# First sequence of a spectral-filter and SwiGLU kernel: filter units moved ahead, last units cut in halves

## The chip, the cores and the metric

The kernel runs on one core of a Trainium2 chip. The metric is the device time of one execution in microseconds; lower is better. Two figures are used side by side: the median of the timed runs, and the time of the one execution that was profiled, whose trace is read here. Times inside the trace count from the start of the profiled span.

Five engines work in parallel, each through its own instructions in order: PE (TensorE, matmuls and transposes by matmul), DVE (VectorE), ACT (ScalarE), POOL (GpSimd) and SP (SyncE). POOL and SP also issue the DMAs of this kernel. PE results land in PSUM banks, which DVE or ACT copy out.

## The reference

For each of 8 sequences of 3008 rows and 256 channels: a real FFT along the sequence, a product with a complex filter, the inverse FFT; then, row by row, an RMS norm and a SwiGLU feed-forward layer with 1536 hidden channels.

```python
X = np.fft.rfft(x, axis=1)
F = (filt_r + 1j * filt_i)[None, :, :]
y = np.fft.irfft(X * F, n=x.shape[1], axis=1)       # 8 x 3008 x 256
x = y.reshape(24064, 256)
rms = np.sqrt(np.mean(x * x, axis=-1, keepdims=True) + 1e-06)
xn = x / rms * rms_g
g = xn @ w_gate                                     # 256 -> 1536
out = (g * (1.0 / (1.0 + np.exp(-g))) * (xn @ w_val)) @ w_out
```

## The kernel before, in words

**The transform.** 3008 is 47 times 64, so the FFT is done in two steps with small tables: step A over 64 points (table `wa`), step B over 47 points with one table for each of 32 residues (`wb`), the filter product, and the same two steps back (`wi`, then `wai`). All are matmuls. Two channel halves of 128 are called `dh`; a "unit" of step B is four residues of one half, so a sequence has 16 units, i = 2g + dh.

**The eight sequences.** The feed-forward work `gv` and `down` (L548 to L565) is a list of 576 items in order. The transforms of sequence b+1 are put between the items of sequence b by a planner with a load table. Sequence 0 has nothing to hide behind: its transform, the loading of the filter and the loading of the weights are written out by hand, in the order in which each engine gets them, and the first item starts after them. The change lies in this hand-written part alone. The planner's items are the same in both kernels.

**The hand-written part, in its order.**

1. POOL issues the DMAs: four for `x` of sequence 0, six of 512 KB for the filter (`f_load`, tile `fs`; for each of three blocks i the imaginary part f=0, then the real part f=1), then `wb` in one call, `wi`, the weights. From the ninth DMA on, each POOL issue waits for the landing of the DMA eight before it. The weights' staging tiles share four buffers with `fs`.
2. Step A: `a0_unit`, six groups for two halves; ACT copies one half from bank tag "pg", DVE the other from "pv". Between them stand `fill` matmuls, whose result is not used, and a transpose of the norm's gain into `gsb`.
3. `tr0_unit(g)`, g = 0 to 7: eight PE transposes and one DVE copy into `t2`. After each of the first seven, one `f_unit`.
4. `f_unit(i, f, dh)`: four PE transposes of one filter tile into a bank, then four copies (five for the last block, i = 2, with one more transpose for the last filter row, tile `tail`) into the filter table `ff`. Twelve units: units 0 to 6 on ACT inside the loop over g, units 7 to 11 behind it, in turn on DVE and ACT. Their order is i, then f, then dh.
5. `f_neg` on POOL writes the negated imaginary part into `ff`, in three pieces, with weight DMAs between them.
6. The loop over p: `b_unit` (PE, banks "mx" and "mb" in turn) and two products `s_part` on DVE with `ff` (L233, L236); two steps later `yt0_unit` (PE, bank "pg", copied out by ACT); two steps later `bi_unit` (PE, bank "pv", copied into `uu` by ACT). For the last unit, i = 15, both copies are on DVE, each of a whole unit, one after the other.
7. `t4_first` transposes the first four row groups of `uu` (PE, copied by ACT and DVE), SP issues the DMA transposes `t4_load`, and `first_norm` computes the first norm: step A back (`psn`), squares on ACT, column sums on PE (`psq`), square root on ACT (`u`), reciprocal on DVE (`rho`), a broadcast by PE (`psr`) and the product `xn` on DVE, in two halves h. Then ACT loads its table for Silu, and item (0, 0, 0) starts. It is itself in two halves.

The waits are made by a framework that watches tiles. It also keeps two engines from touching one PSUM bank at once: in `first_norm` the DVE copy of `psn` waits for the ACT square of the same bank.

Of the kernel before, what the change touches and what calls it, by code (L numbers as in the profile page):

```python
# [12 lines left out]
AXT = mybir.ActivationFunctionType  # L13
# [7 lines left out]
P = 128  # L21
D = 256
# [3 lines left out]
H = 24  # L26
K2 = 32
SL = 48
KR = 2 * SL
# [71 lines left out]
def kernel(  # L101
# [11 lines left out]
    nc = tc.nc  # L113
# [4 lines left out]
    wb_d = nc.inline_tensor(wb_np, name="wb_t").ap()  # L118
# [29 lines left out]
    idf = glob.tile([P, P], FP32)  # L148
    wb = glob.tile([P, K2, KR], FP16)
# [4 lines left out]
    ff = glob.tile([P, 2, K2, 3 * SL], FP32)  # L154
# [3 lines left out]
    gsb = glob.tile([P, 2], FP32)  # L158
    hhs = [glob.tile([P, 512], FP16, name="hh%d" % i) for i in range(4)]
    ss3 = [glob.tile([P, 4, 2, P], FP16, name="ss%d" % i) for i in range(3)]  # L160
    ones = glob.tile([P, 1], FP16)
    epsb = glob.tile([P, 1], FP32)
# [28 lines left out]
    def bank(i, name):  # L191
        pool, tag = ((psM, "mx"), (psG, "pg"), (psV, "pv"), (psB, "mb"))[i]
        return pool.tile([P, 512], FP32, tag=tag, name=name)

    def copy(eng, out, in_, scale=None):
        if eng == "A":
            nc.scalar.activation(out=out, in_=in_, func=AXT.Copy, **({} if scale is None else {"scale": scale}))  # L197
        elif scale is None:
            nc.vector.tensor_copy(out=out, in_=in_)
        else:  # L200
            nc.vector.tensor_scalar(out=out, in0=in_, scalar1=scale, scalar2=None, op0=ALU.mult)
# [77 lines left out]

    done = [0] * B  # L280

    def bi_unit(b, i, eng="A", bk=0):
        g, dh = divmod(i, 2)
        yt = st[b]["yt"][g]
        ps = bank(bk, "psi")[:, 0:4 * KR].rearrange("p (k j) -> p k j", k=4)
        for k in range(4):
            nc.tensor.matmul(ps[:, k, :], yt[0:KR, k, dh, :], wi[0:KR, 4 * g + k, :], start=True, stop=True)  # L287
        dst = uu[:, :, dh, 16 * g:16 * g + 16].rearrange("p c (k m) -> p c k m", k=4)
        copy(eng, dst, ps.rearrange("p k (c m) -> p c k m", c=H))
        done[b] += 1  # L290
        if done[b] == K2 // 2:
            half = uu[:, H - 1, :, :].rearrange("p e (k m) -> p e k m", k=K2)
            if b % 2:
                nc.gpsimd.tensor_copy(out=half[:, :, :, 2:4], in_=left)
            else:
                nc.gpsimd.tensor_copy(out=left, in_=half[:, :, :, 0:2])
# [89 lines left out]
    def f_unit(i, f, dh, e):  # L386
        t = fst[i]
        ps = bank(1 + "AV".index(e), "psf").rearrange("p (a q) -> p a q", a=FR4)
        for a in range(FR4):
            nc.tensor.transpose(ps[:, a, :], t[:, f, a, ds(dh * P, P)], idf)  # L390
        v = ps.rearrange("p a (q s) -> p s a q", s=16)
        fk = ff[:, dh].rearrange("p (t k) c -> p t k c", k=4)
        lo = SL * (1 + f) + 8 * i
        hi = lo + H
        if i < 2:
            copy(e, fk[:, :, :, lo:lo + 8], v[:, 0:8])
            copy(e, fk[:, ::-1, 1:4, hi:hi + 8][:, :, ::-1, :], v[:, 8:16, 1:4, :])
            copy(e, fk[:, 1:8, 0, hi:hi + 8][:, ::-1, :], v[:, 9:16, 0, :])
            copy(e, ff[:, dh, 0, hi:hi + 8], v[:, 8, 0, :])
        else:  # L400
            nc.tensor.transpose(ps[:, 0, 0:1], tail[0:1, f, ds(dh * P, P)], idf[0:1, 0:1])
            copy(e, fk[:, :, :, lo:lo + 8], v[:, 8:16])
            copy(e, fk[:, ::-1, 1:4, hi:hi + 7][:, :, ::-1, :], v[:, 0:8, 1:4, 1:8])
            copy(e, fk[:, 1:8, 0, hi:hi + 7][:, ::-1, :], v[:, 1:8, 0, 1:8])
            copy(e, ff[:, dh, 0, hi:hi + 7], v[:, 0, 0, 1:8])
            copy(e, ff[:, dh, 0, hi + 7:hi + 8], v[:, 0, 0, 0:1])

    def f_neg(k0, n):
        for dh in range(2):
            nc.gpsimd.tensor_scalar(out=ff[:, dh, k0:k0 + n, 0:SL], in0=ff[:, dh, k0:k0 + n, SL:2 * SL],  # L410
                                    scalar1=-1.0, scalar2=1.0, op0=ALU.mult, op1=ALU.mult)

    def yt0_unit(i, eng, bk):
        g, dh = divmod(i, 2)
        s = st[0]["s"].pop(i)[1]
        ps = bank(bk, "psy")[0:KR].rearrange("p (k t) -> p k t", k=4)
        for k in range(4):
            for e in range(2):
                nc.tensor.matmul(ps[:, k, :], s[e][:, k, :], ident, start=(e == 0), stop=(e == 1))  # L419
        if g not in st[0]["yt"]:  # L420
            yt_tile(0, g)
        copy(eng, st[0]["yt"][g][0:KR, :, dh, :], ps)

    def fill(n):
        ps = bank(0, "pf")
        for _ in range(n):
            nc.tensor.matmul(ps, wa, ss3[0].rearrange("p k e q -> p (k e q)")[:, 0:512], start=True, stop=True)

    def t4_first():
        t = xtp.tile([P, 4, D], FP16, tag="xt", name="t4f")  # L430
        for h in range(2):
            ps = psO.tile([P, 2, 2, P], FP16, tag="po%d" % h, name="pst4")
            for q in range(2):
                for dh in range(2):
                    nc.tensor.transpose(ps[:, q, dh, :], uu[:, 2 * h + q, dh, :], ident)
            copy("AV"[h], t[:, 2 * h:2 * h + 2, :].rearrange("p q (e d) -> p q e d", e=2), ps)
        st[0]["t4f"] = t

    def first_norm():
        xn = xnp.tile([P, 4, 2, P], FP16, tag="xn", name="xn")  # L440
        sq = xtp.tile([P, 4, D], FP16, tag="xt", name="sq").rearrange("p (a e) d -> p a (e d)", a=2)
        y = y_tile()
        psn = [bank(1 + h, "psn") for h in range(2)]
        for h in range(2):
            for q in (2 * h, 2 * h + 1):
                for dh in range(2):
                    nc.tensor.matmul(psn[h][:, ts(2 * (q % 2) + dh, P)], st[0]["t4f"][:, q, ds(dh * P, P)], wai,
                                     start=True, stop=True)
            nc.scalar.activation(out=sq[:, h, :], in_=psn[h], func=AXT.Square)
        copy("V", y[:, 0, :], psn[0])  # L450
        fill(1)
        ps = psB.tile([P, 4], FP32, tag="mb", name="psq")
        for q in range(4):
            for dh in range(2):
                nc.tensor.matmul(ps[:, q:q + 1], sq[:, q // 2, ts(2 * (q % 2) + dh, P)], ones,
                                 start=(dh == 0), stop=(dh == 1))
            if q == 1:
                fill(1)
        u = up.tile([P, 4], FP32, tag="u", name="u")
        rho = up.tile([P, 4], FP32, tag="rho", name="rho")  # L460
        nc.scalar.activation(out=u, in_=ps, func=AXT.Sqrt, scale=1.0 / D, bias=epsb)
        nc.vector.reciprocal(out=rho, in_=u)
        copy("A", y[:, 1, :], psn[1])
        fill(2)
        for h in range(2):
            psr = psO.tile([P, 2, P], FP32, tag="po%d" % h, name="psr")
            for q in range(2):
                nc.tensor.transpose(psr[:, q, :], rho[:, 2 * h + q:2 * h + q + 1].to_broadcast([P, P]), idf)
            nc.vector.tensor_tensor(out=xn[:, 2 * h:2 * h + 2],
                                    in0=psr.unsqueeze(2).to_broadcast([P, 2, 2, P]),  # L470
                                    in1=y[:, h, :].rearrange("p (q e t) -> p q e t", q=2, e=2), op=ALU.mult)
        nc.scalar.activation(out=warm, in_=mhalf, func=AXT.Silu)
        fill(2)
        st[0]["xn"][0] = xn

    def n_first(m):
# [135 lines left out]
    with tc.manual_schedule():  # L612
# [12 lines left out]
        nc.sync.dma_start(tail[0:2, 2, 0:P], moe_rms_g.rearrange("(a p) -> a p", p=P))  # L625
        for i in range(3):
            f_load(i)
        nc.gpsimd.dma_start(wb, wb_d)
        nc.gpsimd.dma_start(wi, wi_d)
        w_load(0)  # L630
        w_load(1)
# [7 lines left out]
        def a0(*gqs):  # L639
            for gq in gqs:  # L640
                for dh in range(2):
                    a0_unit(gq, dh, E[dh], 1 + dh)

        a0(0)
        fill(1)
        psg = bank(3, "psg")
        nc.tensor.transpose(psg[:, 0:2], tail[0:2, 2, 0:P], idf[0:2, 0:2])
        copy("V", gsb, psg[:, 0:2])
        fill(1)
        a0(1, 2)  # L650
        fill(2)
        a0(3)
        fill(1)
        a0(4, 5)
        todo = [(i, f, dh) for i in range(3) for f in range(2) for dh in range(2)]
        for g in range(8):
            tr0_unit(g, "V")
            if g < 7:
                f_unit(*todo[g], "A")
        for n, u in enumerate(todo[7:]):  # L660
            f_unit(*u, "VA"[n % 2])
        f_neg(0, 8)
        w_load(2)
        f_neg(8, 8)
# [6 lines left out]
        for q in range(3):  # L671
            w_gain(q)
        UN = K2 // 2
        for p in range(UN + 4):
            if p < UN:
                b_unit(0, p, (0, 3)[p % 2])
                s_part(0, p, 1)
            if 2 <= p < UN + 2:
                yt0_unit(p - 2, "AV"[p - 2 == UN - 1], 1)
            if p >= 4:  # L680
                bi_unit(0, p - 4, "AV"[p == UN + 3], 2)
            if p >= UN + 1:
                fill(1)
        t4_first()
        fill(2)
        for c in range(NXC):
# [166 lines left out]
```

## Time and profile before

| what | value |
| --- | --- |
| timed runs | 871.36, 873.1, 873.5 us; median 873.1 us |
| profiled execution | 872.03 us, span 870.3 us |
| PE busy | 852.1 us, 98% of the span |
| mean granted PE clock | 0.998 |
| first matmul of the first item (L548) | at 47.77 us |

The profiled execution lies 1.07 us under the median, with 1.7 us of it outside the span. PE is busy through nearly the whole span, but not in its first 48 us, which are 5.5% of it: there each engine is at times the one waited for. Reading therefore goes by stages: first the busy time of each engine in each stage, then the order of time inside the stage, asking what the next instruction waited for.

### The profile page before, as it was taken

To read this page: it belongs to the slowest core of one execution; us is meant where nothing else is said; L and a number is where in the kernel's file an instruction comes from. 1 tells how busy PE (TensorE), PEld (TensorE's weight loads), DVE (VectorE), ACT (ScalarE), POOL (GpSimd) and SP (SyncE) were. 2 spreads that over 40 slices of the span, in tenths; PEclk is the share of its full clock that TensorE was granted. 3 is DMA by queue.
4 is the path that set the end of the run, shared out by engine and by line. 5 is a ranking of instruction groups with operands and counts; after the bars stand their busy time and mean duration, and the time that the engine had idled before them with its cause. 6 is when DMAs were issued, how large, how long until landed. Compare 5 with 4: busy or idle time off the path is not lost.

```text
span 870.3 us, 17008 instructions
## 1 busy us (share of the span) xinstructions
PE 852.1 (98%) x6129; PEld 533.0 (61%) x6129; DVE 559.9 (64%) x936; ACT 612.1 (70%) x1352; POOL 295.5 (34%) x340
## 2 busy tenths in 40 slices
PE   6999999999999999999999999999999999999997
PEld 5755666566665566666566666666666666665664
DVE  5856765776666666666576666667666766555554
ACT  4787777787577766877578765788567865777443
POOL 4813841454143421444034430443214440132000
PEclk9999999999999999999999999999999999999999
DMA  9986678655976666744656666634474331522101
GB/s 283 270 149 156 119 152 191 147 117 139 188 146 124 126 134 131 146 110 101 143 120 136 125 124 136 148 87 92 122 142 92 72 91 43 109 67 49 62 25 49
DMA packets 198605, 107.98 MB, mean 124 GB/s; under 512 B 158966, under 2 KB 182904, under 8 KB 198520
## 3 DMA queue, kind: packets, MB, share of 16 engines
q1 hardware_dynamic: 189896, 85.52, 44.4%
q0 software_dynamic: 8480, 21.24, 12.2%
q8 instruction: 48, 0.79, 0.4%
q14 instruction: 37, 0.30, 0.1%
q10 hardware_dynamic: 144, 0.13, 0.0%
HBM read 45.78 MB, written 35.65 MB: 94 GB/s over the span
## 4 chain that ended last, share of the span: by engine, by line
PE 93%; DVE 2%; DMA 2%; ACT 2%; issue 1%; POOL 0%; POOLq 0%; ACTq 0%
PE po L565 27%; PE pg L548 27%; PE pv L548 26%; PE psb L243 3%; PE psi L287 2%; PE psn L316 2%; PE psa L208 2%; DMA xc<-in_x_dram 1%; PE psy L419 1%; DVE hh L553 1%; DMA yt<-ss 1%; ACT sg L552 1%; PE psf L390 1%; ACT uu L197 0%; PE pst L369 0%
## 5 line engine op out<-in xcount | busy, mean ns | idle before, releaser
L553 DVE TENSOR_TENSOR hh<-pv,sg 128x512 f16<-128x512 f32 (+2 forms) x578 | 391.5, 678 | 289.1 <-ACT sg L552 221.7
L552 ACT ACTIVATE sg<-pg 128x512 f16<-128x512 f32 (+2 forms) x578 | 337.7, 585 | 220.1 <-PE pg L548 215.6
L548 PE MATMUL pg<-xn,wg 128*128 128x512 f16 (+2 forms) x1156 | 337.9, 374 | 0.1
L548 PE MATMUL pv<-xn,wv 128*128 128x512 f16 (+2 forms) x1156 | 337.8, 374 | 0.0
L565 PE MATMUL po<-wo,hh 128*128 128x256 f16 x2256 | 332.5, 272 | 0.0
L565 PEld LDWEIGHTS <-hh 128*128 128x128 f16 x2256 | 213.5, 98 | 108.0 <-issue 4.6
L548 PEld LDWEIGHTS <-wv 128*128 128x128 f16 x1156 | 113.0, 98 | 130.6
L270 POOL TENSOR_TENSOR ss<-s,s 128x384 f16<-128x384 f16 x112 | 101.8, 910 | 247.9 <-DVE s L236 220.7
L548 PEld LDWEIGHTS <-wg 128*128 128x128 f16 x1156 | 111.5, 98 | 17.2 <-issue 0.6
L342 POOL TENSOR_TENSOR xt<-y,rho 128x1024 f16<-128x1024 f32 (+1 forms) x46 | 85.3, 1854 | 2.9
L324 ACT ACTIVATE junk<-y 128x256 f16<-128x256 f32 x180 | 74.3, 413 | 2.8
L233 DVE TENSOR_TENSOR s<-psb,ff 128x384 f16<-128x384 f32 x124 | 67.8, 547 | 1.0 <-PE psb L243 0.9
L236 DVE TENSOR_TENSOR s<-psb,ff 128x384 f16<-128x384 f32 x124 | 67.8, 547 | 0.0
L197 ACT ACTIVATE uu<-psi 128x384 f16<-128x384 f32 x127 | 62.0, 489 | 1.9 <-PE psi L287 1.2
L197 ACT ACTIVATE y<-psn 128x512 f32<-128x512 f32 (+1 forms) x95 | 55.7, 588 | 4.3
L332 POOL TENSOR_SCALAR u<-ss 128x4 f32<-128x4 f32 (+1 forms) x46 | 8.8, 192 | 133.8 <-ACT junk L324 133.5
L287 PEld LDWEIGHTS <-yt 96*128 96x128 f16 x512 | 35.5, 98 | 27.9 <-DMA yt<-ss 1.2
L334 POOL TENSOR_TENSOR rho<-u,mhalf 128x4 f32<-128x4 f32 (+1 forms) x46 | 46.4, 1010 | 3.8
L197 ACT ACTIVATE t<-psa 128x512 f16<-128x512 f32 x71 | 42.1, 596 | 3.3 <-PE psa L208 1.7
L287 PE MATMUL psi<-wi,yt 96*128 96x96 f16 x512 | 43.1, 206 | 0.9 <-DMA yt<-ss 0.8
L243 PE MATMUL psb<-wb,t 96*128 96x96 f16 x480 | 40.5, 208 | 1.9 <-DVE s L236 1.7
L243 PEld LDWEIGHTS <-t 96*128 96x128 f16 x480 | 28.9, 98 | 14.4 <-DVE s L236 5.2
(96 smaller groups left out, 364.5 us busy)
## 6 DMA issues: line engine op xcount, KB each, us to landing
out_dram<-o SPq DMA_DIRECT2D x40, 512.0 KB, 3.5
xc<-in_x_dram POOLq DMA_DIRECT2D x31, 384.0 KB, 5.8
z_tmp<-t SPq DMA_DIRECT2D x28, 384.0 KB, 2.7
t<-z_tmp SPq DMA_DIRECT2D x28, 384.0 KB, 6.1
out_dram<-o SPq DMA_DIRECT2D x7, 384.0 KB, 2.7
fs<-in_filt_i_dram POOLq DMA_DIRECT2D x3, 512.0 KB, 11.4
fs<-in_filt_r_dram POOLq DMA_DIRECT2D x3, 512.0 KB, 11.1
ws<-in_moe_w_gate_dram POOLq DMA_DIRECT2D x3, 512.0 KB, 10.9
```

The costliest lines, as they stand in the source:

```text
L197: nc.scalar.activation(out=out, in_=in_, func=AXT.Copy, **({} if scale is None else {"scale": scale}))
L233: eng.tensor_tensor(out=o, in0=ps, in1=f1, op=ALU.mult)
L236: eng.tensor_tensor(out=o, in0=ps[:, :, ::-1, :], in1=f2, op=ALU.mult)
L243: nc.tensor.matmul(ps[:, ts(k, KR)], st[b]["t2"][kk // KC][:, kk % KC, ds(dh * P, P)], wb[0:KR, kk, :], start=True, stop=True)
L270: nc.gpsimd.tensor_tensor(out=ss3[g % 3][:, :, dh, 0:KR], in0=s[0], in1=s[1], op=ALU.add)
L287: nc.tensor.matmul(ps[:, k, :], yt[0:KR, k, dh, :], wi[0:KR, 4 * g + k, :], start=True, stop=True)
L324: nc.scalar.activation(out=junk, in_=y[:, i, ts(u, D)], func=AXT.Square, accum_out=ss[:, 2 * i + u:2 * i + u + 1])
L342: nc.gpsimd.tensor_tensor(out=xt[:, 0:n, :], in0=y.rearrange("p a (u d) -> p (a u) d", u=2)[:, 0:n, :], in1=rho[:, 0:n].unsqueeze(2).to_br ...
L548: nc.tensor.matmul(ps[:, 0:w], wt[:, dt_, ts(jt, P)], xn[:, q0:q1, dt_, :], start=(dt_ == 0), stop=(dt_ == 1))
L552: nc.scalar.activation(out=sg[:, c], in_=pg[:, 0:w], func=AXT.Silu)
L553: nc.vector.tensor_tensor(out=hh[:, c], in0=pv[:, 0:w], in1=sg[:, c], op=ALU.mult)
L565: nc.tensor.matmul(po[s4 // 2][:, s4 % 2, :], hh[:, ts(s4, P)], wo[:, jt, :], start=(jt == 0 and s4 % 2 == 0), stop=(jt == JT - 1 and (s4 ...
```

## The change

Only the first sequence is touched.

- Two `f_unit`s are issued after step A and ahead of `tr0_unit(0)`; the loop over g then carries units 2 to 8, and units 9, 10, 11 follow it on DVE, ACT, ACT. The last block's order is now dh, then f: both parts of half 0 come before half 1.
- The last filter row is transposed earlier, in step A, into the bank that also takes the gain; one DVE copy puts it into `ff`. `f_unit` loses that transpose and a copy.
- `wb` is loaded by two calls, 16 residues each. One more DMA stands on POOL's queue.
- Unit 15 of `yt0_unit` and of `bi_unit` is cut into two halves of two residues, one copied by DVE and one by ACT. The copy of `bi_unit` 13 moves from ACT to DVE. One `fill` goes, and the two that remain use bank "pg".
- `t4_first` copies its first half on DVE and its second on ACT (before: the other way round).
- `first_norm` takes sums, square root and reciprocal by halves. The fills are placed anew: 2, 1, 1 and 3 of them from `t4_first` on, before 2, 1, 1, 2 and 2.

```diff
-    def bi_unit(b, i, eng="A", bk=0):
+    def bi_unit(b, i, eng="A", bk=0, ks=slice(0, 4)):
...
-        for k in range(4):
+        for k in range(4)[ks]:
...
-        copy(eng, dst, ps.rearrange("p k (c m) -> p c k m", c=H))
-        done[b] += 1
+        copy(eng, dst[:, :, ks], ps.rearrange("p k (c m) -> p c k m", c=H)[:, :, ks])
+        done[b] += ks.stop == 4
...
         else:
-            nc.tensor.transpose(ps[:, 0, 0:1], tail[0:1, f, ds(dh * P, P)], idf[0:1, 0:1])
...
-            copy(e, ff[:, dh, 0, hi + 7:hi + 8], v[:, 0, 0, 0:1])
...
-    def yt0_unit(i, eng, bk):
+    def yt0_unit(i, eng, bk, ks=slice(0, 4)):
...
-        copy(eng, st[0]["yt"][g][0:KR, :, dh, :], ps)
+        copy(eng, st[0]["yt"][g][0:KR, ks, dh, :], ps[:, ks])
...
-            copy("AV"[h], t[:, 2 * h:2 * h + 2, :].rearrange("p q (e d) -> p q e d", e=2), ps)
+            copy("VA"[h], t[:, 2 * h:2 * h + 2, :].rearrange("p q (e d) -> p q e d", e=2), ps)
...
         copy("V", y[:, 0, :], psn[0])
-        fill(1)
         ps = psB.tile([P, 4], FP32, tag="mb", name="psq")
-        for q in range(4):
-            for dh in range(2):
-                nc.tensor.matmul(ps[:, q:q + 1], sq[:, q // 2, ts(2 * (q % 2) + dh, P)], ones,
-                                 start=(dh == 0), stop=(dh == 1))
-            if q == 1:
-                fill(1)
...
-        nc.scalar.activation(out=u, in_=ps, func=AXT.Sqrt, scale=1.0 / D, bias=epsb)
-        nc.vector.reciprocal(out=rho, in_=u)
+        for h in range(2):
+            fill(1)
+            c = slice(2 * h, 2 * h + 2)
+            for q in range(2 * h, 2 * h + 2):
+                for dh in range(2):
+                    nc.tensor.matmul(ps[:, q:q + 1], sq[:, h, ts(2 * (q % 2) + dh, P)], ones,
+                                     start=(dh == 0), stop=(dh == 1))
+            nc.scalar.activation(out=u[:, c], in_=ps[:, c], func=AXT.Sqrt, scale=1.0 / D, bias=epsb)
+            nc.vector.reciprocal(out=rho[:, c], in_=u[:, c])
         copy("A", y[:, 1, :], psn[1])
-        fill(2)
...
-        fill(2)
+        fill(3)
...
-        nc.gpsimd.dma_start(wb, wb_d)
+        for h in range(2):
+            nc.gpsimd.dma_start(wb[:, ts(h, K2 // 2), :], wb_d[:, ts(h, K2 // 2), :])
...
         a0(0)
-        fill(1)
+        fill(2)
+        a0(1, 2)
         psg = bank(3, "psg")
-        nc.tensor.transpose(psg[:, 0:2], tail[0:2, 2, 0:P], idf[0:2, 0:2])
-        copy("V", gsb, psg[:, 0:2])
-        fill(1)
-        a0(1, 2)
+        for f in range(2):
+            for dh in range(2):
+                nc.tensor.transpose(psg[:, 2 * dh + f:2 * dh + f + 1], tail[0:1, f, ds(dh * P, P)], idf[0:1, 0:1])
+        nc.tensor.transpose(psg[:, 4:6], tail[0:2, 2, 0:P], idf[0:2, 0:2])
+        copy("V", ff.rearrange("p e k (s q) -> p e k s q", s=3)[:, :, 0, 1:3, SL - 1],
+             psg[:, 0:4].rearrange("p (e s) -> p e s", e=2))
+        copy("V", gsb, psg[:, 4:6])
         fill(2)
         a0(3)
         fill(1)
         a0(4, 5)
-        todo = [(i, f, dh) for i in range(3) for f in range(2) for dh in range(2)]
+        todo = [(i, f, dh) for i in range(2) for f in range(2) for dh in range(2)]
+        todo += [(2, f, dh) for dh in range(2) for f in range(2)]
+        f_unit(*todo[0], "A")
+        f_unit(*todo[1], "A")
         for g in range(8):
             tr0_unit(g, "V")
             if g < 7:
-                f_unit(*todo[g], "A")
-        for n, u in enumerate(todo[7:]):
-            f_unit(*u, "VA"[n % 2])
+                f_unit(*todo[g + 2], "A")
+        for n, u in enumerate(todo[9:]):
+            f_unit(*u, "VAA"[n])
...
-        for p in range(UN + 4):
+        for p in range(UN + 3):
...
-            if 2 <= p < UN + 2:
-                yt0_unit(p - 2, "AV"[p - 2 == UN - 1], 1)
-            if p >= 4:
-                bi_unit(0, p - 4, "AV"[p == UN + 3], 2)
-            if p >= UN + 1:
-                fill(1)
+            if 2 <= p < UN + 1:
+                yt0_unit(p - 2, "A", 1)
+            if p == UN + 1:
+                yt0_unit(UN - 1, "V", 1, slice(0, 2))
+                yt0_unit(UN - 1, "A", 0, slice(2, 4))
+            if 4 <= p < UN + 3:
+                bi_unit(0, p - 4, "AV"[p == UN + 1], 2)
+            if UN + 1 <= p < UN + 3:
+                fill(1, 1)
+        bi_unit(0, UN - 1, "V", 3, slice(0, 2))
+        bi_unit(0, UN - 1, "A", 0, slice(2, 4))
```

More of the change, by code (lines that the diff above doesn't have):

```diff
@@ L411, in f_neg @@
                                     scalar1=-1.0, scalar2=1.0, op0=ALU.mult, op1=ALU.mult)
-    def yt0_unit(i, eng, bk):
+    def yt0_unit(i, eng, bk, ks=slice(0, 4)):
         g, dh = divmod(i, 2)
-        s = st[0]["s"].pop(i)[1]
+        s = st[0]["s"][i][1]
         ps = bank(bk, "psy")[0:KR].rearrange("p (k t) -> p k t", k=4)
-        for k in range(4):
+        for k in range(4)[ks]:
             for e in range(2):
@@ L421, in yt0_unit, with fill @@
             yt_tile(0, g)
-        copy(eng, st[0]["yt"][g][0:KR, :, dh, :], ps)
-    def fill(n):
-        ps = bank(0, "pf")
+        copy(eng, st[0]["yt"][g][0:KR, ks, dh, :], ps[:, ks])
+    def fill(n, bk=0):
+        ps = bank(bk, "pf")
         for _ in range(n):
```

## The prediction

> **What bounds the kernel now.** First the page: busy time by engine, and the chain that ended last.
>
> ```profile
> PE 852.1 (98%) x6129; PEld 533.0 (61%) x6129; DVE 559.9 (64%) x936; ACT 612.1 (70%) x1352; POOL 295.5 (34%) x340
> ...
> PE 93%; DVE 2%; DMA 2%; ACT 2%; issue 1%; POOL 0%; POOLq 0%; ACTq 0%
> ```
>
> PE bounds the whole, and nothing of its later work is changed. So what the first sequence saves before its first item moves everything behind it. Where that part is bound, the table by stage tells (length, then busy time of PE, PE's loads, DVE, ACT, POOL; then clock, DMA share, GB/s):
>
> ```profile
> 0.00:14.00 14.00, 6.10 (x55) 4.42 (x55) 5.81 (x14) 4.96 (x8) 7.33 (x17) 1.00 0.87 209
> 14.00:25.10 11.10, 10.50 (x123) 9.62 (x123) 8.15 (x24) 7.14 (x38) 4.50 (x8) 1.00 1.02 409
> 25.10:40.60 15.50, 14.31 (x229) 13.34 (x229) 15.06 (x33) 11.84 (x27) 15.43 (x24) 0.89 1.16 271
> 40.60:47.80 7.20, 6.17 (x59) 3.38 (x60) 3.35 (x8) 5.25 (x11) 0.70 (x2) 1.00 0.78 147
> 47.80:72.00 24.20, 24.20 (x163) 14.56 (x163) 13.75 (x24) 20.41 (x42) 2.83 (x4) 1.00 0.75 152
> ```
>
> Filter stage: PE 10.50 of 11.10. Product stage: DVE 15.06 of 15.50. Between 40.6 and 47.8 no engine is full: a chain of waits, padded on PE with fills. After that PE has no gap. The order of time (start, length, engine, line) gives the waits:
>
> ```profile
> 15.22 6.12 ACT L197 ACTIVATE ff<-psf 128x256 f32<-128x256 f32 x28 [1.56 <-PE psf L390]
> ...
> 24.24 0.92 DVE L199 COPY ff<-psf 128x256 f32<-128x256 f32 x5 [0.56 <-PE psf L401]
> ...
> 25.07 0.55 DVE L233 TENSOR_TENSOR s<-psb,ff 128x384 f16<-128x384 f32 x1
> ...
> 26.14 0.34 PE L243 MATMUL psb<-wb,t 96*128 96x96 f16 x4 [1.49 <-DVE s L236]
> ...
> 30.20 0.56 DVE L233 TENSOR_TENSOR s<-psb,ff 128x384 f16<-128x384 f32 x1 [0.41 <-PE psb L243]
> ...
> 41.39 0.69 DVE L199 CAST yt<-psy 96x512 f16<-96x512 f32 x1 [0.75 <-PE psy L419]
> ...
> 42.52 0.56 DVE L199 CAST uu<-psi 128x384 f16<-128x384 f32 x1 [0.44 <-PE psi L287]
> ...
> 46.80 1.28 ACT L472 ACT_TABLE_LOAD   x1
> 47.03 1.29 DVE L469 TENSOR_TENSOR xn<-psr,y 128x512 f16<-128x512 f32 x2 [0.53 <-PE psr L468]
> ```
>
> ACT waits 1.56 us before its first filter copy; the products start at 25.07, when the last filter copy, on DVE, ends. One more row, from PE's second-by-second windows (the clock is the second number from the brackets on):
>
> ```profile
> 28.00:29.00 1.00, 1.00 (x14) 0.50 1.03 389
> ```
>
> PE ran at half clock from about 27.4 to 30.9, after the gap of 1.49 us at 26.14, and the DVE wait of 0.41 at 30.20 follows from it.
>
> **Filter stage.** The first filter load is issued at 3.63 and lands 9.8 later, 13.43. Step A leaves PE at 13.2, and its ACT copies end at 13.67. So unit 0 can start on PE at 13.5, unit 1 at 13.93, and `tr0_unit(0)` at 14.36, when `uu` is complete (DVE ends at 14.09). Unit 0 was on PE from 14.52 and its copies began at 15.22; the same 0.70 gives 14.2. Unit 2 needs unit 0's bank, free after copies of 0.87 (6.12 / 7): 15.1. From there each turn (one unit, one `tr0_unit`) has PE's old period, 0.89 (16.69, 17.58, 18.47): unit 8 at 15.1 + 6 x 0.89 = 20.44, `tr0_unit(7)` at 20.87, units 9, 10, 11 at 21.32, 21.75, 22.18, unit 0 of step B at 22.61, its bank full 0.38 later, 23.0. The five moved last-row transposes (0.15 each in the chain, four of them here) leave this stretch; in step A they and one copy like that of `gsb` (0.16) lie in the wait for `x` (0.51 at 12.26), or cost 0.3 without it. The two fills of step A that now stand together are the same two; the gain's transpose that stood between them waited 0.28 for its load and no longer does. DVE copies `tr0_unit(7)` from 21.50 to 22.19 and then unit 9, at most 0.87: 23.06. The first product needs half 0 alone, since the last block now goes by half, and starts at 23.1 instead of 25.07: **2.0 saved**. Bounds: 1.6 (landing seen by POOL only at 13.76, and a little on DVE) to 2.2.
>
> Covers. Unit 11's copies on ACT end at 23.95, needed at 23.1 + 0.93 = 24.0. `f_neg` follows unit 10 on POOL and ends at 23.8, needed at 24.5. Behind it stand two weight DMAs (0.76 and 0.73), then the second piece (0.99): 26.3, needed by unit 4 at 27.3; the third, 28.8 against 31.0. POOL's issues now wait for one DMA later, because `wb` is two; the one ahead of the second piece waits for the first half of `wb`, there by 23.05. The extra issue is 0.53 of POOL's idle time. `wb` landed at 10.65 + 12.4 = 23.05, after 22.61: whole, it would cost 0.4. Its first half lands between 21.4 (half of the 3.2 us since the last filter load at 19.84) and 23.05: 0 to 0.4, taken as 0, since queue and bytes are in order. Were a cover missing, its lateness would be paid in full on DVE.
>
> **Product stage.** 32 products at a spacing of 0.463: 31 x 0.463 + 0.54 = 14.9, from 25.07 to 39.96. The trace ends at 40.63: 0.67 belongs to the half clock. Now PE's idle stretch ahead of the third `b_unit` runs from about 23.0 to 24.1, 1.1 against 1.49, and the clock's stretches of 3.4 us hold more work around it. In the stretch before the drop (24.02 to 27.44) PE was busy 1.8 us, 52%; the least busy one that kept its clock (10.37 to 13.78) had about 70%. With the same phase the new ones have 69% and 73%. I take the drop as gone: **0.67 saved**; bounds 0 and 0.67. The Trainium skill ("TensorE: Matmul & The Clock Gate", Why this matters for your kernels) says that only PE gaps over about 3 us cost the clock; the trace shows a drop after gaps of half that. By that rule a shorter gap would change nothing and the sum would be rival 1's.
>
> **Last unit.** From the last product's end to the first transpose of `uu`: 40.63 to 43.13, 2.50. Now four matmuls fewer before the first half's copy (4 x 0.056): copy from 0.54, 0.42 long (128x256 rows: 0.42; ends between 0.34 and 0.69). ACT has two whole copies ahead (to 0.86), then its half to 1.23, `uu` of unit 14 to 1.78, its last half (128x192 rows: 0.33) to 2.12. DVE: unit 13 to 1.52, half to 2.0. PE starts at 2.17: **0.33 saved**. ACT sets it; moving unit 13 to DVE is what keeps it from 2.6.
>
> **First norm**, from that transpose on. Before: squares end at 2.55, `u` starts at 2.90, `rho` at 3.20, the first `xn` runs from 3.90 to 4.58, and the second half of the first item starts on PE at 5.24. Now: DVE's half of `t4f` is ready at 0.80 (ACT's was at 0.98), squares at 1.28 and 1.82, ending at 2.36. `u` of half 0 follows to 2.62 (0.26, as for four columns). Half 1's sums wait for it, since both lie in one bank: 2.67; its `u` from 2.95 to 3.21, `rho` to 3.43, first `xn` to 4.13, second to 4.75. Three fills (0.65) end at 4.33 on PE. Second half of the item: 4.80, 0.44 earlier. ACT: `y`, then the table load from 3.72 to 5.0, first Silu at 5.10, against 5.07. So ACT gains nothing here; the second step-A matmul waits for its copy. I take **0.35**; bounds 0 and 0.44.
>
> **Sum.** 2.0 + 0.67 + 0.33 + 0.35 = 3.35; 872.03 - 3.35 = 868.68. The profiled run lies 1.07 under the median: 869.75, said as 869.7.
>
> **Rivals.**
> 1. The half clock stays: the phase of the stretches is not known, and from 22.3 to 25.7 PE would be about half busy. 0.67 less: 870.4.
> 2. The gain runs into DMA. `x` of sequence 1 loads until 42.3 (197 GB/s up to 42, 61 after). `t4_load` was issued at 43.17 into idle queues and would now be at 40.2. Its second block is issued 1.75 later and lands after 4.0: 5.8 after the transposes, needed at 7.4. With the slowest landing of that line, 7.1, it is 1.45 late: 871.2.
> 3. Nothing arrives: the saved time returns as a wait for weights or `x`. 873. Against it: the weights land by 37, POOL's scaling ends at 41, and the first third that the first items need by 36.
> 4. Slower: the clock drops in the filter stage, which is transposes alone from 13.5 to 22.6 and PE's own bound. A half-clock stretch of 3.4 us costs 1.7 there; from two on the gain is gone, three give 869.7 + 5.1 = 874.8. Against it: 14 to 25.1 has clock 1.00. The Trainium skill (same page, Part 4: PE-mode transpose) says that transposes do not count as PE work in the same way; by that rule this rival would hold, and the trace of before disagrees.
>
> **How the numbers follow.** Forecast 0.42; rival 1 0.22, rival 2 0.17, rival 3 0.10, rival 4 0.09. What a measurement here tells from no change is 0.3%, 2.6 us: faster means under 870.5. That takes 0.39 of the forecast, 0.12 of rival 1 (870.4 lies on the line) and 0.03 of rival 2: 0.54. Slower is rival 4, 0.09; the rest is 0.37. The range runs from 868.3 (bounds 2.2 and 0.44 used) to 872.2, over rivals 1 and 2 and a part of 3.
>
> **What would show it.** First filter copy near 14.2; first product near 23.1; no clock of 0.50 and no DVE wait between; last product 14.9 after the first; transposes of `uu` 2.2 later; second half of the first item 4.8 after these; no wait of `psn` (L485 before) for `t`. Wrong if the first unit waits for the filter long after 13.5, if DVE waits for POOL in the first eight units, or if `xn` is early but PE then waits for ACT.

## The result, and the profile after

The changed kernel takes 868.86 us in the median of six runs (868.79 to 869.87). The kernel before, on the same chip, takes 872.75 us in six (871.14 to 873.5). The ratio is 0.9964, interval 0.9952 to 0.9976: faster by 0.36%. The forecast was 869.7 us and the range 868.3 to 872.2.

The profiled execution of the changed kernel is the longest of its six, 869.87 us, with a span of 868.1; the forecast for a profiled run was 868.68. So the trace shows a gain of 2.2 us where the medians show 3.9. First the page of the changed kernel, busy time by engine:

```profile
PE 852.2 (98%) x6127; PEld 533.1 (61%) x6127; DVE 558.8 (64%) x929; ACT 614.5 (71%) x1360; POOL 296.0 (34%) x341
```

PE's work is the same (852.1 before). Next, the table by stage of the changed kernel (stretch, length, busy time of PE, PE's loads, DVE, ACT, POOL; clock, DMA share, GB/s):

```profile
0.00:14.00 14.00, 7.80 (x55) 5.95 (x56) 4.99 (x14) 4.47 (x7) 7.65 (x17) 1.00 0.86 207
14.00:24.10 10.10, 10.09 (x126) 9.79 (x123) 7.41 (x15) 8.28 (x42) 3.40 (x5) 1.00 1.03 411
24.10:39.00 14.90, 13.55 (x229) 11.89 (x229) 14.90 (x32) 12.97 (x32) 14.73 (x23) 1.00 1.15 283
39.00:45.40 6.40, 5.72 (x57) 3.46 (x58) 3.64 (x10) 5.14 (x13) 2.66 (x5) 1.00 1.16 196
45.40:72.00 26.60, 26.32 (x175) 15.73 (x174) 14.83 (x26) 22.27 (x47) 3.74 (x6) 1.00 0.78 166
```

Every stage between 14 us and the first item is shorter, the product stage has clock 1.00 instead of 0.89, and PE is idle for 0.28 us in the last stretch, where it had no gap before. The order of time in the changed kernel (a code line has other numbers than before: L433 and L482 were L435 and L485):

```profile
12.63 1.91 PE L359 MATMUL psa<-wa,xc 128*128 128x128 f16 x16
...
15.16 7.62 ACT L197 ACTIVATE ff<-psf 128x256 f32<-128x256 f32 x36 [0.41 <-PE psf L390]
...
24.06 0.56 DVE L233 TENSOR_TENSOR s<-psb,ff 128x384 f16<-128x384 f32 x1
...
25.14 0.34 PE L243 MATMUL psb<-wb,t 96*128 96x96 f16 x4 [1.04 <-DVE s L236]
...
40.85 0.81 PE L433 MATMUL pst<-ident,uu 128*128 128x128 f16 x8 [0.19 <-ACT uu L197]
41.05 8.57 SPq L301 DMA_TRANSPOSE t<-uu  x4
...
49.18 0.40 PE L482 MATMUL psn<-wai,t 128*128 128x128 f16 x4 [0.28 <-DMA t<-uu]
...
49.41 0.60 PE L562 MATMUL po<-wo,hh 128*128 128x256 f16 x4
```

From these rows come the lengths used from here on, in microseconds. "First product" is the first row of L233, "product stage" runs from it to the end of the last product, "last unit" from there to the transposes of `uu` on PE, "norm" from these to the second half of the first item, "to down" from there to the first `down` matmul (`po`). The transposes are counted from the second of the eight, because before, the first ran alone, 0.59 ahead of the others; in the changed kernel the second starts at 41.11.

| kernel | first filter copy | first product | product stage | last unit | norm | to down | first down at | span |
| --- | --- | --- | --- | --- | --- | --- | --- | --- |
| before | 15.22 | 25.07 | 15.57 | 2.50 | 5.23 | 3.04 | 51.41 | 870.3 |
| after | 15.16 | 24.06 | 14.96 | 2.09 | 4.72 | 3.59 | 49.41 | 868.1 |

So the profiled run saved 1.01 + 0.61 + 0.41 + 0.51 and gave back 0.55: 1.99 (2.00 by the rounded rows). From the first `down` to the end of the span it is 818.7 after and 818.9 before: what the first sequence saves goes through whole.

Two things differ from the forecast: a first product at 24.06 instead of 23.1, and a wait for `t`, which the prediction had named as a sign against it. The wait is rival 2's. PE stood idle for 0.28 of it; its weight loads waited 0.45, and by that much `psn` took longer. The bytes per second of the changed kernel (last number) show what it collides with:

```profile
41.00:42.00 1.00, 0.97 (x11) 0.56 (x11) 0.42 (x1) 0.32 (x2) 0.66 (x2) 1.00 1.06 209
42.00:43.00 1.00, 0.96 (x10) 0.46 (x9) 0.00 (x0) 0.90 (x3) 0.00 (x0) 1.00 1.64 197
43.00:44.00 1.00, 0.81 (x10) 0.55 (x11) 0.81 (x2) 0.67 (x3) 0.00 (x0) 1.00 0.73 62
```

`x` of sequence 1 loads until 43, and the DMA transposes of `t` start at 41.05, into that load. Before, they started at 43.17, when it had ended. The kernel before:

```profile
43.17 7.03 SPq L301 DMA_TRANSPOSE t<-uu  x4
...
51.41 0.60 PE L565 MATMUL po<-wo,hh 128*128 128x256 f16 x4
```

The second of the four transposes is the one that `psn` needs. It was issued at 44.77 before and landed 4.1 later, at 48.9; in the changed kernel it was issued at 43.59 and landed 5.5 later, at 49.1. It was issued 1.2 earlier and landed no earlier, while PE wanted it 2.45 earlier (`psn` at 48.51 instead of 50.96).

### The profile page after: what moved, and what is told of

It is laid out like the page before. It is cut to its first block, busy times and chain, and to the rows that moved or that the text cites. A ratio compares the mean times of both kernels' runs of the same rounds, so it can differ in the third digit from the quotient of the medians.

```text
span 868.1 us, 17009 instructions
## 1 busy us (share of the span) xinstructions
PE 852.2 (98%) x6127; PEld 533.1 (61%) x6127; DVE 558.8 (64%) x929; ACT 614.5 (71%) x1360; POOL 296.0 (34%) x341
## 4 chain that ended last, share of the span: by engine, by line
PE 93%; DMA 2%; ACT 2%; DVE 2%; issue 1%; POOL 0%; SPq 0%; DVEq 0%; POOLq 0%; ACTq 0%
PE po L562 27%; PE pg L545 27%; PE pv L545 26%; PE psb L243 3%; PE psi L287 2%; PE psn L316 2%; PE psa L208 2%; DVE hh L550 1%; ACT sg L549 1%; DMA yt<-ss 1%; DMA xc<-in_x_dram 1%; PE psf L390 1%; DMA t<-uu 1%; PE psy L417 1%; ACT uu L197 1%
## 5 line engine op out<-in xcount | busy, mean ns | idle before, releaser
L233 DVE TENSOR_TENSOR s<-psb,ff 128x384 f16<-128x384 f32 x124 | 67.9, 548 | 0.6 <-PE psb L243 0.3
L197 ACT ACTIVATE uu<-psi 128x384 f16<-128x384 f32 (+1 forms) x127 | 61.4, 485 | 1.9 <-PE psi L287 1.0
```

The lines of the kernel that those rows point to most:

```text
L233: eng.tensor_tensor(out=o, in0=ps, in1=f1, op=ALU.mult)
```

## The experiments

The theory under test was the prediction's sum with rival 2 added: each stage gives its own term, and an early `t4_load` costs a part of it. The rivals: the filter stage is bound by something else, the half clock has another cause or costs nothing, and the `t` wait does not come from the load of `x`. Each kernel was also timed beside the kernel before on the same chip: 872.1 us for the first four below (22 runs of it), 871.64 for the next four (17 runs), 872.09 for the last four (18 runs).

**The filter stage alone.** The kernel before with the new order of step A (the last filter row in it) and of the filter units, its table in one call and its old tail. The main part of the edit:

```diff
+        todo = [(i, f, dh) for i in range(2) for f in range(2) for dh in range(2)]
+        todo += [(2, f, dh) for dh in range(2) for f in range(2)]
+        f_unit(*todo[0], "A")
+        f_unit(*todo[1], "A")
...
-                f_unit(*todo[g], "A")
-        for n, u in enumerate(todo[7:]):
-            f_unit(*u, "VA"[n % 2])
+                f_unit(*todo[g + 2], "A")
+        for n, u in enumerate(todo[9:]):
+            f_unit(*u, "VAA"[n])
```

> The kernel before with the filter stage of the change alone (units ahead, last block by half, last row in step A; the table in one call, the tail as before). The sum on record: first product near 23.1 to 23.5 (the whole table lands at 23.05), no half-clock stretch, 2.2 to 2.7 us faster than before. The rival, that the clock's rise in step A decides: where PE is cold until about 15 us, the first product comes near 24.1 and only 1.0 to 1.7 us is gained; where it rises near 10 or 11, 2.2 to 2.7.

869.3 us (869.06 to 869.55), ratio 0.9969 (0.9957 to 0.9981). The order of time of this kernel:

```profile
14.01 7.62 ACT L197 ACTIVATE ff<-psf 128x256 f32<-128x256 f32 x36 [0.28 <-PE psf L390]
...
22.93 0.56 DVE L233 TENSOR_TENSOR s<-psb,ff 128x384 f16<-128x384 f32 x1 [0.17 <-PE psb L243]
...
48.67 0.23 PEld L483 LDWEIGHTS <-t 128*128 128x128 f16 x4 [0.24 <-DMA t<-uu]
```

Copies at 14.01 and first product at 22.93, where the prediction had 14.2 and 23.1. The product stage is 14.97 at full clock. This part alone gives 2.8 us by the medians, a little over the 2.2 to 2.7 expected. Its transposes of `t` start at 40.42, and already PE's loads wait 0.24 for them.

**The rest without the filter stage.** The changed kernel with the filter stage, the step-A order and the table call of before; only the halves of the last unit and of the first norm stay:

```diff
-        todo += [(2, f, dh) for dh in range(2) for f in range(2)]
-        f_unit(*todo[0], "A")
-        f_unit(*todo[1], "A")
...
-        for n, u in enumerate(todo[9:]):
-            f_unit(*u, "VAA"[n])
+        for n, u in enumerate(todo[7:]):
+            f_unit(*u, "VA"[n % 2])
```

> The change without its filter stage and with the table in one call: halves of the last unit and of the first norm alone. The sum on record: 0.7 us faster (0.33 + 0.35). If the wait of psn for t, seen in the changed kernel, comes from the transfers of x that end near 43 us, it is absent here, because the transposes start at about 42.7 as they nearly did before, and 0.8 to 0.9 is kept; if it comes from the shorter way from the transposes to psn, it is here too, and 0.3 is left.

871.57 us (870.06 to 872.32, eleven runs), ratio 0.9991 (0.9983 to 1.0). The median is 0.5 lower, hardly clear of noise. Last unit 2.10 and norm 4.71, as in the changed kernel: 0.92 saved. But its profiled span, 870.4, is that of before, since its first filter copy came at 16.74 and its first product at 26.59, 1.5 late; the next experiment bears on that. There was no wait for `t`, though the way from the transposes to `psn` is as short as in the changed kernel: the DMA transposes started at 44.03, when the load of `x` was nearly over (172 GB/s from 43 to 44, 43 from 44 to 45). So the wait does not come from the shorter way. "To down" was 3.13, so 0.09 of what the changed kernel gave back there is not the wait. The half clock was there again. Its window at 28:

```profile
28.00:29.00 1.00, 1.00 (x14) 0.50 0.91 352
```

**The changed kernel with eight more fills ahead of step A.** The durations in step A had differed between profiles: the sixteen matmuls at 12.63 in the changed kernel above took 1.91 us. This tests whether PE's start is what made it lose 1 us against the forecast.

```diff
+        fill(8)
         a0(0)
```

> The changed kernel with 8 fills ahead of step A, while PE waits for x. If the clock's rise decides the filter stage: full clock by 8 to 11 us in every run, step A off PE by 13.3, first filter copy near 14.2, first product near 23.1, and 0 to 1.1 us less than the changed kernel, depending on the phase of its runs. If step A waits for x in any case: no change. If the fills delay step A: up to 0.5 us more.

868.9 us (868.68 to 869.05), ratio 0.9964 (0.9951 to 0.9976). The order of time of this kernel:

```profile
14.02 7.62 ACT L197 ACTIVATE ff<-psf 128x256 f32<-128x256 f32 x36 [0.60 <-PE psf L390]
...
48.32 0.40 PE L482 MATMUL psn<-wai,t 128*128 128x128 f16 x4 [0.56 <-DMA t<-uu]
```

The first product is at 22.91, 1.15 earlier than in the profile of the changed kernel, but the first `down` comes at 48.55, only 0.86 earlier: the wait for `t` grew from 0.28 to 0.56. The runs lie within 0.37 us of each other; the median is that of the changed kernel in its own set, so the fills show in the trace and not in the time. Against the filter stage alone, on the same chip, the median is 0.4 lower; the back part saves 0.93 in the rows and `t` takes the larger part of it.

**The load of `x` moved into the transposes.** Two of the four loads of `x` of sequence 1 leave the hand-written part and are issued with the first item:

```diff
-        for c in range(NXC):
+        for c in range(2):
...
+        at(0, x_load, 1, 2)
+        at(0, x_load, 1, 3)
```

> The changed kernel with the last two of the four loads of x of the next sequence issued with the first items instead of ahead of the weights' scaling. If the transposes of t are slowed by these loads: the issue of the four transposes takes 7 us as before instead of 8.6, psn (L482 in the changed kernel) does not wait for t, and 0.4 to 0.5 us is gained. If not: the wait of 0.45 stays. Against it: step A of the next sequence could wait for x, for 0 to 2 us.

873.42 us (871.66 to 875.68), ratio 1.0014 (1.0003 to 1.0024). It was expected to gain 0.4 to 0.5, with half of the load out of the transposes' way. It came out 1.3 above the kernel before instead: the planner put both issues at 40.49, right behind the start of the transposes:

```profile
39.98 12.02 SPq L301 DMA_TRANSPOSE t<-uu  x4
40.49 1.22 POOL L188 DMA_DIRECT2D xc<-in_x_dram  x2 [0.17 <-issue]
...
51.23 0.61 PE L482 MATMUL psn<-wai,t 128*128 128x128 f16 x4 [3.41 <-DMA t<-uu]
```

Issuing the four transposes took 12.02 us, against 8.57 in the changed kernel and 7.03 before, and PE waited 3.41. So it is shown directly that loads beside the transposes make them late, and here the wait eats the whole gain. The profile also has a half-clock stretch from 51.26 on, after that wait, which adds 1.3 behind it (820.0 from the first `down` to the end).

**The step that waits, one item later.** Instead of moving the DMA, the planner's marks for the second norm are each moved by one item, so that `psn` stands behind one more item of PE work:

```diff
-        at(2, n_first, 1)
-        at(4, q_unit, 1)
-        at(6, scale_split, 1)
-        at(8, scale_apply, 1, 3)
+        at(3, n_first, 1)
+        at(5, q_unit, 1)
+        at(7, scale_split, 1)
+        at(9, scale_apply, 1, 3)
```

(The load marks of the same items move by one too.)

> The changed kernel with psn of the second norm block and the steps after it one item later (items 3, 5, 7, 9 instead of 2, 4, 6, 8). If the wait for the transposes of t is what takes back a part of the gain: no wait of PE there, the first down matmul 3.1 after the second half of the first item instead of 3.6, and 0.4 to 0.8 us less. If something else is late there, it stays.

868.28 us (868.01 to 868.57 in five runs and 871.93 in the sixth), ratio 0.9965 (0.9951 to 0.9978). In the order of time of this kernel, `down` comes first and `psn` then runs its eight matmuls without a wait:

```profile
47.61 0.60 PE L562 MATMUL po<-wo,hh 128*128 128x256 f16 x4
...
48.91 0.61 PE L482 MATMUL psn<-wai,t 128*128 128x128 f16 x8
```

Its span is 866.3. Since `psn` no longer stands ahead of the first `down`, it is the span that compares: 867.2 in the kernel of the same set that has `psn` in its old place (the table in one call, below), 868.96 in the median. With the eight fills on top:

> The same, and 8 fills ahead of step A. If both waits are independent: full clock by 11 us, first product near 22.9, no wait for t, 0.4 to 0.9 us under the changed kernel's median and under the run with the norm block one item later by 0 to 0.3; spread of the runs under 0.5 us.

868.0 us (867.8 to 868.44), ratio 0.9956 (0.9944 to 0.9967), span 866.1, first `down` at 47.56.

**The table in one call.** The changed kernel with the single load of `wb` of before:

```diff
-        for h in range(2):
-            nc.gpsimd.dma_start(wb[:, ts(h, K2 // 2), :], wb_d[:, ts(h, K2 // 2), :])
+        nc.gpsimd.dma_start(wb, wb_d)
```

> The changed kernel with the table loaded in one call, as before. The sum on record: 0 to 0.4 us slower, since the whole table landed at 23.05 and step B's first matmuls want it at 22.6. From the trace of the filter stage alone, where the whole table was used and the first product still began at 22.93: no difference.

868.96 us (868.69 to 869.15), ratio 0.9966 (0.9953 to 0.9979). The row that the two calls remove, in this kernel:

```profile
22.64 0.37 PEld L243 LDWEIGHTS <-t 96*128 96x128 f16 x8 [0.15 <-DMA wb<-wb_t]
```

The wait exists, but it is at most 0.15, and by the medians the split is worth nothing that can be told. The first product came at 23.09 here and at 22.91 with the split (the kernel with fills); 0.12 of this stood already in the first filter copy, at 14.14 against 14.02.

**The gap filled, nothing else.** The kernel before, with five fills where PE waited 1.49 us:

```diff
+            if p == 2:
+                ps = bank(1, "pf")
+                for _ in range(5):
+                    nc.tensor.matmul(ps, wa, ss3[0].rearrange("p k e q -> p (k e q)")[:, 0:512], start=True, stop=True)
```

> The kernel before with 5 fills on PE in the idle stretch ahead of the third step-B unit (24.6 to 26.1). If the half-clock stretch comes from that idle stretch: no clock of 0.50 until the end in nearly all runs, no DVE wait of 0.41, last product 15.0 after the first instead of 15.6, and 0.6 to 1.2 us off the median. By the rule that only gaps over about 3 us count: the stretch of half clock stays and nothing is gained.

871.54 us (870.98 to 872.52, eleven runs), ratio 0.9998 (0.999 to 1.0007). The order of time, then the window at 28, of this kernel:

```profile
24.61 1.24 PE L678 MATMUL pf<-ss,wa 128*128 128x512 f16 x5
...
26.27 0.34 PE L243 MATMUL psb<-wb,t 96*128 96x96 f16 x4 [0.41 <-DVE s L236]
```

```profile
28.00:29.00 1.00, 0.88 (x16) 1.00 1.02 385
```

The drop is gone in this profile, and the product stage is 14.94 instead of 15.57. In the medians nothing of this is seen, where 0.6 to 1.2 was expected. The mean granted clock, which is on record for every timed run, helps here. The half clock of the profile before lasted 3.4 us (27.2 to 30.6), which lowers the mean of a run by 0.002 (3.4 x 0.5 / 870), so a run that reads 1.000 had none. Of 57 runs of the kernel before, six read 1.000 and took 871.2 in the median; the 33 that read 0.998 or less took 872.6. With the gap filled, nine of eleven read 1.000 and took 871.43. So the drop is in some executions of the kernel before and not in others, and where it is missing the fills gain nothing. How often it is there cannot be counted from the mean, which a half clock behind the last matmul lowers too (the profiled run of the copy below reads 0.998, with clock 1.00 up to its last matmul); so its price in the median stays open. The same reading helps the rest without the filter stage: its four runs at 1.000 took 870.06 to 870.78, below all six of the kernel before (870.94 to 871.8).

**The changed kernel again, beside its own variants.** A copy of the changed kernel, timed in one set with the following three:

> The changed kernel once more, beside the others of this set. 868.7 to 869.0 in most runs; first product at 22.9 to 23.1 where the clock rises by 12 us, 24.1 where it rises later; PE waits 0.3 to 0.8 us for the transposes of t.

869.18 us (868.65 to 870.46), ratio 0.9969 (0.9958 to 0.9979). The order of time of this copy, its DMA transposes among it:

```profile
12.00 1.11 PE L359 MATMUL psa<-wa,xc 128*128 128x128 f16 x16
...
13.86 7.62 ACT L197 ACTIVATE ff<-psf 128x256 f32<-128x256 f32 x36 [0.35 <-PE psf L390]
...
22.83 0.56 DVE L233 TENSOR_TENSOR s<-psb,ff 128x384 f16<-128x384 f32 x1 [0.21 <-PE psb L243]
...
39.83 9.49 SPq L301 DMA_TRANSPOSE t<-uu  x4
...
48.71 0.40 PE L482 MATMUL psn<-wai,t 128*128 128x128 f16 x4 [1.04 <-DMA t<-uu]
```

The same kernel, and another split of the loss: the sixteen matmuls take 1.11 instead of 1.91, the first product is at 22.83, and PE waits 1.04 for `t`, more than the 0.3 to 0.8 expected. The second transpose was issued at 42.26 and landed 6.4 later, at 48.7. The first `down` comes at 48.95; in the kernel with the filter stage alone it came at 48.91. In this profile the halves of the last unit and of the norm, 0.93 in these rows, end in that wait whole; in the other profiles with the whole filter stage 0.3 to 0.6 of them was left.

The version with the later norm and the fills, again:

> The kernel with 8 fills ahead of step A and the second norm block one item later, once more, for a comparison on one chip: 0.6 to 1.0 us under the changed kernel. If the difference between the earlier sets was the chip's, under 0.3.

868.18 us (867.94 to 869.82), ratio 0.9961 (0.9949 to 0.9974): 1.0 us under the changed kernel in the same set. In its profiled run the first filter landed late: PE's first filter transposes waited 0.39 for it and began at 14.18, and the first product came at 23.75.

**The two halves of the filter change.** The changed kernel with the last block in the old order (i, f, dh):

```diff
-        todo = [(i, f, dh) for i in range(2) for f in range(2) for dh in range(2)]
-        todo += [(2, f, dh) for dh in range(2) for f in range(2)]
+        todo = [(i, f, dh) for i in range(3) for f in range(2) for dh in range(2)]
```

> The changed kernel with the last filter block's units in the old order, part before half. By the sum's steps the first product then waits for the copies of unit 10 on ACT, which end near 23.2 instead of unit 9's on DVE near 23.0: first product 0.2 to 0.4 later, 869.0 to 869.3. If the order is what carries the gain: about 1 us.

869.1 us (868.83 to 869.95), ratio 0.9967 (0.9956 to 0.9979). And without the two units ahead:

```diff
-        f_unit(*todo[0], "A")
-        f_unit(*todo[1], "A")
...
-                f_unit(*todo[g + 2], "A")
-        for n, u in enumerate(todo[9:]):
-            f_unit(*u, "VAA"[n])
+                f_unit(*todo[g], "A")
+        for n, u in enumerate(todo[7:]):
+            f_unit(*u, "VA"[n % 2])
```

> The changed kernel without the two units ahead: units 0 to 6 in the loop, 7 to 11 behind it in turn on DVE and ACT, last block by half. DVE then copies unit 11 ahead of the first product, as in the kernel before, but without its four last-row transposes: first product near 24.5, 1.5 later than in the changed kernel, 870.0 to 870.6. If the units ahead only moved a wait: under 0.5 later.

869.72 us (869.12 to 870.64), ratio 0.9974 (0.9965 to 0.9983). The first product of the one with the old order, then of the one without units ahead:

```profile
23.11 0.56 DVE L233 TENSOR_TENSOR s<-psb,ff 128x384 f16<-128x384 f32 x1 [0.23 <-ACT ff L197]
```

```profile
21.84 2.53 DVE L199 COPY ff<-psf 128x256 f32<-128x256 f32 x12
...
24.29 0.55 DVE L233 TENSOR_TENSOR s<-psb,ff 128x384 f16<-128x384 f32 x1
...
25.35 0.34 PE L243 MATMUL psb<-wb,t 96*128 96x96 f16 x4 [1.53 <-DVE s L236]
```

The old order makes DVE wait 0.23 for ACT's last copies; in time it is not to be told from nothing, because the wait for `t` (0.54 here against 1.04 in the copy) takes the difference up. Without the units ahead the first product is 1.46 later than in the copy, and DVE has three units to copy at the end. Of that, 0.5 reaches the median, less than expected (869.72 against 870.0 to 870.6): `psn` waits for `t` only 0.1 here, so the copy gives most of its lead back. By the first product, the units ahead are the main part of the filter stage's gain, 1.46 of 2.24. The last row bears on the half clock: PE's gap is as long as before, 1.53, and yet this profile keeps clock 1.00. Four of this kernel's eleven runs read a mean clock of 0.997.

## Why the prediction was right, by its steps

| step | forecast saved | profile of the changed kernel | copy of the changed kernel |
| --- | --- | --- | --- |
| filter stage | 2.0 (1.6 to 2.2) | 1.01 | 2.24 |
| product stage | 0.67 (0 to 0.67) | 0.61 | 0.61 |
| last unit | 0.33 | 0.41 | 0.41 |
| first norm | 0.35 (0 to 0.44) | 0.51 | 0.52 |
| wait for `t` and what follows it | 0, rival 2 up to -1.45 | -0.55 | -1.31 |
| sum, first `down` | 3.35 | 1.99 | 2.47 |

**Filter stage.** Right: with the units ahead, wherever the sixteen matmuls ran at full rate or nearly so and the first loads were in time, the first product came between 22.83 and 23.11, forecast 23.1. The covers that it named held: none of the products waited for POOL. What it left out is that step A can leave PE later. The prediction took 13.2 from a single profile; in the changed kernel's profile step A ended at 14.54 (12.63 + 1.91), because PE still ran slowly until then, and 1.0 us of the stage's gain (24.06 against 23.1) went there. The kernel with the old filter stage had the same in its profile (first product 1.5 later than before), so this loss is not the change's own: it depends on the execution.

**Product stage.** The term was right in the trace: the new stage ran in 14.94 to 14.97 us with clock 1.00, in all eleven profiles with the new filter stage or a part of it, and in the one with the gap filled; in both profiles of the old stage the clock dropped. The gap is 1.49 in these two, 1.0 to 1.1 in ten of the eleven. But it does not decide alone, since the kernel without the units ahead kept its clock in its profile with a gap of 1.53: the same kernel drops in some executions and not in others. The mean clocks say how the gap counts. Under 0.998 lie 11 of 57 runs of the kernel before, 7 of 11 with the old filter stage and the new end, 4 of 11 without the units ahead, 1 of 51 of the kernels with the shorter gap (the run at 871.93; the kernel with the moved load is not counted) and none of 11 with the gap filled. So rival 1 did not come true, but what the term is worth in the median is not settled: the kernel that filled the gap gained nothing there. Why one execution drops and another does not was not tested, and neither was the prediction's busy share of PE (52% ahead of the drop). The rule of the Trainium skill ("TensorE: Matmul & The Clock Gate", Why this matters for your kernels), to leave no gaps of over about 3 us between bursts of matmuls, does not cover this trace: here the drop follows a gap of 1.49.

**Last unit and first norm.** Right, each a little undersized (by 0.08 and 0.16). Of the norm's 0.51, about 0.1 is lost again on the way to `down`, as the kernel without the new filter stage shows (3.13 against 3.04, with no wait for `t`); its cause is open. The table counts it in the row of the wait.

**Rival 2.** It had 0.17 and came true in part, beside the forecast and not in place of it. The step that failed is the sum itself, which let the transposes of `t` move 3 us forward at no cost. Rival 2 says why: it has the second transpose land 5.8 after the start of the first, as in the idle queues of before, and `psn` needs it at 7.4. Measured, it landed 8.0 after the start in the changed kernel and 8.8 in the copy. The cost to `down`: 0.55 where the transposes started at 41.05, and 0.83 (with the fills) and 1.31 (the copy) where they started near 40, about 0.1 of each from elsewhere. The forecast's own earlier start was 40.2. Its size was bounded well (1.45); its chance was too low: the wait stands in all seven profiles that have the units ahead and leave `psn` in its place.

**Rivals 3 and 4.** The weights were not late, so the saved time did arrive; and PE's stretch of transposes alone, from 14.7 to 23.4 us, kept clock 1.00 (it lies in the second row of the table by stage) and 219 ns for a 128x128 transpose. The rule of the Trainium skill ("TensorE: Matmul & The Clock Gate", Part 4: PE-mode transpose) that transposes do not count as PE work in the same way is not what this trace shows.

**The sum.** In the trace the saving is 0.9 to 1.4 under the forecast, in the changed kernel's profile for both reasons above, in the copy for the wait alone; in the medians it is 3.89 in the first set and 2.91 in the last, around the 3.35. The profiled run lay 1.0 above its median this time, where the prediction had added 1.07 for a profiled run below it. That the time came out 0.8 below the forecast rests on this offset and not on a step of the sum: the profiled time was missed by 1.2 one way, the offset by 2.1 the other way, and that the two nearly cancel is luck. The lower end of the range is luck too. It is 872.03 less the upper bounds of the four terms, 3.64, which gives 868.39, and it leaves out the 1.07 that the forecast and the rivals carry; with it the end would be 869.46, and 868.86 lies below that.

## What to carry to other kernels

When a hand-written start gets shorter, ask of each DMA that moves forward with it what will be loading at its new time; here 0.4 to 1.2 us of what was saved ended in a wait for transposes that had been issued into idle queues before. Moving the instruction that waits by one item of PE work was worth 1.0 us with eight fills ahead (against the copy) and 0.7 without (against the kernel with the table in one call), and needed no faster DMA. And a term of under 1 us ought to be read from several profiles: start and clock of PE, and the first DMA, each moved by about that much between executions of one kernel.

## What the runs showed of the hardware

- PE's slow start has no fixed length: sixteen matmuls of step A took 1.91 us in one execution of the changed kernel and 1.11 in another. The granted clock reads 1.00 throughout, so only the durations tell it (314 ns against 219 for the same 128x128 matmul). By these, full rate came at about 14.7 and 11.5 in the two, and at 6.9, 7.9 and 11.6 in the three profiles with eight fills ahead.
- DMA transposes slow down when loads run beside them: issuing four took 7.03 us with the loads over (7.71 and 7.86 in two other kernels), 8.37 to 9.64 with the loads of `x` still ending, 12.02 with two more loads issued into them. An earlier start hardly brought them in earlier: the second of the four landed at 48.9, 49.1 and 48.7 when the first started at 43.17, 41.05 and 39.83.
- A half clock can follow a short gap of PE, and need not: 3.4 us at 0.50 in two profiles with a gap of 1.49, none in one with 1.53, none in ten with 1.0 to 1.1. A run's mean clock tells some executions apart that one profile cannot.
